# An adaLN + S4D + token-mixing block on one core: the first token block's late values come from SBUF, squares are taken from the sum, and the last gate moves to the activation

## The chip, the core and the metric

The kernel runs on one core of a Trainium2 chip. The metric is the device time of one execution, in microseconds; the runs shown for a kernel give a median. Engines are named as in the profile: PE (TensorE, with PEld for its weight loads), DVE (VectorE), ACT (ScalarE), POOL (GpSimd) and SP (SyncE). SPq is the queue of DMAs that SP issues.

## What is computed

All arrays are float32. `x` has 2048 tokens of 448 channels. The part of the reference that matters here:

```
mod = (_silu(c) @ w_mod)...          # six rows of 448: sa, ca, ga, sb, cb, gb
h = _layernorm(x) * (1 + ca) + sa
x = x + ga * _A_ref(h, ...)          # per-channel long convolution, by FFT
h = _layernorm(x) * (1 + cb) + sb
x = x + gb * _B_ref(h, ...)          # token mixing

def _B_ref(x, w1, b1, w2, b2):
    h = _layernorm(x, axis=-1)                  # again, over channels
    u = _gelu(einsum("bsd,sf->bdf", h, w1) + b1)   # 2048 tokens -> 1792
    y = einsum("bdf,fs->bds", u, w2) + b2          # 1792 -> 2048 tokens
    return y.transpose(0, 2, 1)
```

So there are two layer norms in a row for each token (the modulated one, then the plain one of `_B_ref`), and `gb` multiplies the output of the second product, bias included.

## The kernel before

**Stages.** The convolution is done with DFTs of length 4096, factored as 64 x 64, as matmuls. The kernel generation and the transforms of the input fill the first half of the time. What matters here is the end of the second stage and all of the third.

**End of stage two (lines 763 to 828 and 1170 to 1200).** The spectrum is multiplied and transformed back in 32 pieces `n = 0..31`. Pieces 0 to 15 make the first half of the channels (224 columns, `DC`), pieces 16 to 31 the second half. Each piece gives two of the 32 rows `k` of a table `v_d` in DRAM, `[32, 128, 448]`. For one piece: `pc_load` loads the signal's spectrum `u` and a table `si`; `pc_s2` is two matmuls (`kx`); `pc_mul` multiplies on DVE (`z`); `pc_inv` is four matmuls with the inverse tables (`vv`, L820 and L821); `pc_out` copies `vv` from PSUM to an SBUF tile `vt` on ACT (L826) and writes it to `v_d` (L828). In the loop at L1172, `pc_out` of piece `n - 1` follows the matmuls of piece `n`.

The 128 partitions of a piece's `vv` are 128 combinations of the token index. The tables `I1`, `I2` of `dft_tables` fix their order; before, it is `(ch, g, r)` with `ch` of 4, `g` of 2 and `r` of 16.

**Stage three, first product (L1203 to L1328).** Tokens are handled in 16 blocks `r` of 128. `ln_load(r)` loads from `v_d` what belongs to block `r` (a tile `vt` of 128 partitions, which are the 32 rows `k` and 4 `ch`, by 2 `g` by 448; L1230). `ln_y(r)` is the last transform, two matmuls with the table `ft` into PSUM tile `y` (L1250; there is one such buffer), and adds it to the residual on DVE with the row sum as by-product (L1253, `total`). `stats` gives the mean on DVE (L1240), the sum of squared differences on ACT (L1242, `Square` with the negated mean as bias) and the root on ACT (L1243). `ln_mod` applies the first norm and the modulation on DVE (L1260 to L1262), calls `stats` again, and `ln_out` applies the second norm (L1267 to L1280). Its result is split in two float32r tiles, `h3h` and `h3l`, whose sum is the value. `mlp1` multiplies them with the weights, also split (`whi`, `wlo`): three matmuls for each of seven slices of 128 hidden units (L1222 to L1224), into seven PSUM accumulators. That is done for the first 896 hidden units (parts 0 to 15) and then for the other 896 (parts 16 to 31).

**Weights.** `WeightStream` brings each part of the weights: `load` issues the raw load on SP (three raw buffers), `begin` casts it to `whi` on ACT (L206), `rest` makes `wlo` on DVE (L215). Parts 0 and 1 are prepared at L1199, before the first block is touched; their instructions stand ahead of block 0's in the queues of ACT and DVE.

**After each half (`gelu`, L1332).** Seven times: gelu on ACT from the accumulator into a tile `u` (three buffers; L1336), a cast to `uh` on DVE (L1337), the remainder `ul` on DVE (L1338).

**Second product (L1353 to L1370).** For each of 16 blocks of tokens, 42 matmuls into `o`, those on the first half's `uh` and `ul` first (L1364 to L1366). Then DVE adds `b2` and multiplies by `mod[5]`, which is `gb` (L1368), adds the residual (L1369), and SP stores the block.

**Order.** On PE, ACT, DVE and POOL the order is the written order in all that is described here. SP's queue is ordered by a planner until L1188, which is passed after piece 27 has been written; from there to L1328 its DMAs, too, are issued in the written order. A DMA that has to wait holds up those behind it on the same queue. Matmuls on `mod[3]` that nothing reads (`warm`) stand before each of the first three steps of the loop at L1296: nine, one and two.

## Time and profile before

| | us |
|---|---|
| median of 3 runs | 700.01 |
| the runs | 700.01, 697.52, 702.35 |
| the profiled execution's own time | 699.5 |
| its span, first to last instruction | 697.7 |
| PE busy in it | 646.5 |
| ACT, DVE, POOL busy | 448.5, 424.1, 274.7 |
| mean granted TensorE clock | 0.988 |
| DMA, over the span | 128.04 MB, 184 GB/s |

A row of the timeline reads: start, duration (us), engine, line, operation, tiles written and read, shape, count, and in brackets how long the engine was idle before and what ended that. In the chain of waits a row is start, duration and what took it; a DMA row runs from its issue to its landing. In a row of the windows the first number after the stretch is its length, then come the busy times of PE, PEld, DVE, ACT and POOL, the granted clock, the busy share of the DMA engines and the GB/s moved. A float32 matmul shows as two records.

### The profile page before, as it was taken

The page shows a single profiled execution, that of the slowest core. Times are in us where ns is not written, and L with a number is a line of the kernel's source. Part 1 is how long each engine was busy: PE and PEld are TensorE (multiplying, and loading weights), DVE is VectorE, ACT ScalarE, POOL GpSimd, SP SyncE. Part 2 cuts the span into 40 slices and gives each one's busy share as a digit, 9 for nine tenths or more (in the row PEclk, how much of TensorE's full clock was granted, in tenths as well). Part 3 has the DMA queues.
Part 4 walks back from the last instruction along what each step waited for, and adds up shares of the span by engine and source line. Part 5 has one row for each costly group of instructions (what it writes and reads, how often), then busy time and mean ns, then how long its engine had stood idle before and what let it go on. Part 6 is the DMA issues. An engine that isn't in the chain of part 4 may idle for free.

```text
span 697.7 us, 18532 instructions
## 1 busy us (share of the span) xinstructions
PE 646.5 (93%) x7314; PEld 486.1 (70%) x7314; DVE 424.1 (61%) x811; ACT 448.5 (64%) x841; POOL 274.7 (39%) x364
## 2 busy tenths in 40 slices
PE   0868999999988899999999989999999999999997
PEld 0444454455545676676789747778999999999996
DVE  7877889787575584857744368777622354444431
ACT  5787698899879899999766568877422332222220
POOL 6694669588588767777546200000000000000000
PEclk9998999999999999999999999999999999999999
DMA  7595647588785486554579899974683445555640
GB/s 183 178 194 143 214 163 241 212 234 268 213 266 165 126 170 170 145 157 120 142 235 301 257 278 244 236 177 135 174 247 108 146 132 159 159 158 165 169 129 28
DMA packets 101894, 128.04 MB, mean 184 GB/s; under 512 B 13547, under 2 KB 85231, under 8 KB 101807
## 3 DMA queue, kind: packets, MB, share of 16 engines
q1 hardware_dynamic: 100606, 123.31, 63.0%
q0 software_dynamic: 1200, 3.54, 2.4%
q8 instruction: 58, 0.95, 0.6%
q14 instruction: 30, 0.24, 0.1%
HBM read 91.46 MB, written 34.87 MB: 181 GB/s over the span
## 4 chain that ended last, share of the span: by engine, by line
PE 68%; ACT 10%; DMA 8%; DVE 6%; issue 4%; POOL 3%; SPq 1%; DVEq 0%; ACTq 0%; POOLq 0%
PE xe L621 7%; PE acc L1222 7%; PE o L1365 6%; PE o L1364 6%; PE o L1366 6%; PE acc L1223 6%; PE acc L1224 6%; PE kg L711 6%; DMA si<-in_SK_dram 3%; PE xg L621 3%; PE pu L542 2%; PE pu L574 2%; PE vv L820 2%; PE kx L804 2%; PE vv L821 2%
## 5 line engine op out<-in xcount | busy, mean ns | idle before, releaser
L206 ACT CAST whi<-w 128x896 fp32r<-128x896 f32 x64 | 59.8, 938 | 134.9 <-PE o L1365 84.6
L215 DVE TENSOR_TENSOR wlo<-w,whi 128x896 fp32r<-128x896 f32 x64 | 68.1, 1088 | 43.1 <-ACT whi L206 36.8
L684 POOL TENSOR_TENSOR G<-mag,gs 128x512 f32<-128x512 f32 x56 | 71.9, 1283 | 50.9 <-ACT gs L680 47.1
L1222 PE MATMUL acc<-h3h,whi 128*128 128x448 f32 x224 | 82.7, 369 | 0.8 <-ACT h3h L1273 0.8
L1223 PE MATMUL acc<-h3l,whi 128*128 128x448 f32 x224 | 81.5, 364 | 0.7 <-DVE h3l L1280 0.5
L1365 PE MATMUL o<-ul,whi 128*128 128x448 f32 x224 | 81.3, 363 | 0.0
L1364 PE MATMUL o<-uh,whi 128*128 128x448 f32 x224 | 81.2, 362 | 0.0
L1224 PE MATMUL acc<-h3h,wlo 128*128 128x448 f32 x224 | 80.7, 360 | 0.0
L1366 PE MATMUL o<-uh,wlo 128*128 128x448 f32 x224 | 80.6, 360 | 0.0
L711 PEld LDWEIGHTS kg<-E,G 128*32 128x32 f32 x3584 | 56.6, 114 | 32.3 <-issue 22.2
L711 PE MATMUL kg<-E,G 128*32 128x64 f32 x3584 | 66.4, 228 | 6.7 <-issue 6.1
L685 POOL TENSOR_TENSOR G<-mag,gs 128x512 f32<-128x512 f32 x56 | 71.8, 1282 | 0.0
L621 PE MATMUL xg<-tab,lph 64*128 64x512 f32 x112 | 62.3, 556 | 5.1 <-ACT gs L680 2.4
L621 PE MATMUL xe<-tab,lph 64*128 64x512 f32 x112 | 62.2, 555 | 1.1 <-ACT gs L681 0.9
L686 DVE TENSOR_TENSOR E<-m,xe 128x512 f32<-128x512 f32 x53 | 36.4, 687 | 41.3 <-ACT xe L679 24.3
L1368 DVE SCALAR_TENSOR_TENSOR y<-o,b,mod 128x448 f32<-128x448 f32 x16 | 10.9, 684 | 80.2 <-PE o L1366 80.2
L665 POOL TENSOR_TENSOR m<-mag,w 128x512 f32<-128x512 f32 x53 | 56.0, 1056 | 4.3 <-DMA u<-us_d 0.2
L1222 PEld LDWEIGHTS acc<-h3h,whi 128*128 128x128 f32 x224 | 42.0, 188 | 13.9 <-ACT h L1278 5.6
L812 DVE TENSOR_TENSOR z<-kx,u 128x448 f32<-128x448 f32 x48 | 28.4, 620 | 27.7 <-PE kx L804 27.7
L1223 PEld LDWEIGHTS acc<-h3l,whi 128*128 128x128 f32 x224 | 42.1, 188 | 3.3 <-DVE h3l L1280 0.8
L1364 PEld LDWEIGHTS o<-uh,whi 128*128 128x128 f32 x224 | 42.0, 188 | 3.4
L621 PE MATMUL xe<-tab,lex 64*128 64x512 f32 x56 | 28.9, 531 | 16.6 <-DMA lex<-wm 15.8
(233 smaller groups left out, 1512.1 us busy)
## 6 DMA issues: line engine op xcount, KB each, us to landing
w<-in_B_w_dram SPq DMA_DIRECT2D x64, 224.0 KB
w<-in_B_w_dram SPq DMA_DIRECT2D x32, 448.0 KB
u<-us_d SPq DMA_DIRECT2D x48, 224.0 KB
yu_d<-yt SPq DMA_DIRECT2D x16, 448.0 KB
yi<-yu_d SPq DMA_DIRECT2D x32, 224.0 KB
us_d<-uo SPq DMA_DIRECT2D x16, 448.0 KB
v_d<-vt SPq DMA_DIRECT2D x32, 224.0 KB
vt<-v_d SPq DMA_DIRECT2D x16, 448.0 KB
```

The lines of the kernel that those rows point to most:

```text
L206: self.nc.scalar.copy(hi, w)
L215: eng.tensor_tensor(lo, w, hi.bitcast(F32), ALU.subtract)
L621: T.matmul(out[k], lhs[r], rhs[r], start=start, stop=stop)
L684: G.tensor_tensor(Gt[:, 1], mg_, v32(sg), ALU.mult)
L685: G.tensor_tensor(Gt[:, 0], mg_, v32(cg_), ALU.mult)
L711: T.matmul(kg[32 * q : 32 * q + 32, m], Gt[:, c, d], E[:, c, d], start=h == 0 and c == 0 and m == 0, stop=h == 1 and c == 1, skip_group_ch ...
L1222: nc.tensor.matmul(acc[f], hi[:, fs], h3h[:, r], start=r == 0, stop=False)
L1223: nc.tensor.matmul(acc[f], hi[:, fs], h3l[:, r], start=False, stop=False)
L1224: nc.tensor.matmul(acc[f], lo[:, fs], h3h[:, r], start=False, stop=r == 15)
L1364: nc.tensor.matmul(o, hi[:, ks], uh[kh][:, k], start=kh == 0 and k == 0, stop=False)
L1365: nc.tensor.matmul(o, hi[:, ks], ul[kh][:, k], start=False, stop=False)
L1366: nc.tensor.matmul(o, lo[:, ks], uh[kh][:, k], start=False, stop=kh == 1 and k == 6)
```

## The change

There are four parts.

1. *The order of a piece's rows.* `I1` and `I2` are permuted so that the partitions of `vv` are `(r, ch, g)`. The eight rows of one block and one `k` now lie side by side in `v_d`, and the load of a block reads, for each partition, two neighbouring rows in one run (`v_load`).
2. *Block 0.* Its `vt` is loaded in stage two, in parts: two small loads bring the first-half columns of rows `k = 28..31` after piece 28 has been written (they lie there since pieces 14 and 15); at the loop's step 15 a load brings all columns of rows 0 to 27, which includes piece 29, and stands on SP before the writes of pieces 30 and 31. The second-half columns of rows 28 to 31 come from the SBUF tiles of pieces 30 and 31: four small copies, issued on ACT, put them in `vlast` (16 partitions). `ln_y(0)` becomes six matmuls of 224 columns: two over 128 rows, two over 112 rows, and two with the table `fl` over the 16 rows of `vlast`. `ln_load(0)` at the start of stage three is gone. The warm-up matmuls become two, three and one.
3. *Squares from the sum.* `Square` takes the sum as bias and scales its input by -448, so that the result is 448 squared times as large; `Sqrt` scales back. The mean is still made on DVE, and is no longer an input of the square.
4. *The gate.* `u` is multiplied by `mod[5]` on DVE right after each gelu. In the second half the cast to `uh` moves to ACT, one slice late. After the second product, `b2 * mod[5]` and the residual are joined without `o`, and `o` is added last.

```diff
-    order = lambda a: a.reshape(P, 32, 2, 2, 2, 16).swapaxes(3, 4)
+    order = lambda a: a.reshape(P, 32, 2, 2, 2, 16).transpose(0, 1, 5, 2, 4, 3)
...
+    t["FL"] = ft[-16:].reshape(2, 2, 4, 64).swapaxes(1, 2).reshape(16, 64)
...
             nc.sync.dma_start(rows.rearrange("k p d -> p k d"), vt)
+            if n >= 2 * NP - 2:
+                q = 8 * (n % 2)
+                for g in range(2):
+                    nc.scalar.dma_start(vlast[q : q + 8, g], vt[g:8:2])
...
+        v_v = v_d.rearrange("k (r ch g) d -> r k ch g d", ch=4, g=2)
+        end = 2 * NP - 4
+        vlast = swp.tile([16, 2, DC], F32, name="vlast", bufs=1)
+        fl = swp.tile([16, 64], F32, name="fl", bufs=1)
+        nc.sync.dma_start(fl, i["FL"])
+        vts = {}
+
+        def v_load(r, k):
+            nc.sync.dma_start(vts[r][0 : 4 * k].rearrange("p g d -> p (g d)"), v_v[r, 0:k].rearrange("k ch g d -> k ch (g d)"))
...
+            if k == NP - 1:
+                v_load(0, end)
             if k:
                 pc_inv(n - 1)
                 pc_out(n - 1)
...
             if k == NP - 3:
                 wst.load()
                 x_pair(0)
+                vts[0] = rot.tile([P, 2, D], F32, tag="vt", name="vt", bufs=4)
+                for g in range(2):
+                    nc.sync.dma_start(vts[0][4 * end :, g, 0:DC], v_v[0, end:, :, g, 0:DC])
...
-        v_v = v_d.rearrange("k (ch g r) d -> r (k ch) g d", ch=4, g=2)
...
-            nc.sync.dma_start(vts[r], v_v[r])
+            v_load(r, 2 * NP)
...
-            V.tensor_scalar(mean, total, -1.0 / D, None, ALU.mult)
             sq = rot.tile([P, D], F32, tag="sq", name="sq")
-            S.activation(sq, src, AF.Square, bias=mean, accum_out=ss)
-            S.activation(rs, ss, AF.Sqrt, scale=1.0 / D, bias=eps_t)
+            S.activation(sq, src, AF.Square, bias=total, scale=-float(D), accum_out=ss)
+            S.activation(rs, ss, AF.Sqrt, scale=1.0 / D**3, bias=eps_t)
+            V.tensor_scalar(mean, total, -1.0 / D, None, ALU.mult)
...
+                if r:
+                    nc.tensor.matmul(out, ft, vt[:, g], start=True, stop=True)
+                    continue
+                n = 4 * end
+                nc.tensor.matmul(out[:, 0:DC], ft, vt[:, g, 0:DC], start=True, stop=True)
+                nc.tensor.matmul(out[:, DC:], ft[0:n], vt[0:n, g, DC:], start=True, stop=False)
+            if r == 0:
+                for g in range(2):
+                    nc.tensor.matmul(y[64 * g : 64 * g + 64, DC:], fl, vlast[:, g], start=False, stop=True)
...
-        for r in range(4):
+        for r in range(1, 4):
             ln_load(r)
...
-                warm((9, 1, 2)[t + 3])
+                warm((2, 3, 1)[t + 3])
...
         def gelu(acc, fh):
+            us = {}
+
+            def split(f, copy):
+                copy(uh[fh][:, f], us[f])
+                V.tensor_tensor(ul[fh][:, f], us[f], uh[fh][:, f].bitcast(F32), ALU.subtract)
+
             for f in range(7):
                 k = 7 * fh + f
-                u = ru.tile([P, D], F32, tag="u", name="u")
-                S.activation(u, acc[f], AF.Gelu_apprx_tanh, bias=b1[:, k : k + 1])
-                V.tensor_copy(uh[fh][:, f], u)
-                V.tensor_tensor(ul[fh][:, f], u, uh[fh][:, f].bitcast(F32), ALU.subtract)
+                us[f] = ru.tile([P, D], F32, tag="u", name="u")
+                S.activation(us[f], acc[f], AF.Gelu_apprx_tanh, bias=b1[:, k : k + 1])
+                V.tensor_tensor(us[f], us[f], mod[5], ALU.mult)
+                if fh == 0:
+                    split(f, V.tensor_copy)
+                elif f:
+                    split(f - 1, S.copy)
+            if fh:
+                split(6, S.copy)
...
-            V.scalar_tensor_tensor(y, o, b2[:, t : t + 1], mod[5], ALU.add, ALU.mult)
-            V.tensor_tensor(y, y, xt, ALU.add)
+            V.scalar_tensor_tensor(xt, mod[5], b2[:, t : t + 1], xt, ALU.mult, ALU.add)
+            V.tensor_tensor(y, o, xt, ALU.add)
```

9 lines of the change are left out of this document (5 added, 4 removed).

## The prediction

> **What bounds the kernel now.** I read the page first, then the chain of waits, and then the timeline engine by engine between 384 and 420 us, where the second stage hands over to the mixer block.
>
> ```profile
> PE 646.5 (93%) x7314; PEld 486.1 (70%) x7314; DVE 424.1 (61%) x811; ACT 448.5 (64%) x841; POOL 274.7 (39%) x364
> PE 68%; ACT 10%; DMA 8%; DVE 6%; issue 4%; POOL 3%; SPq 1%; DVEq 0%; ACTq 0%; POOLq 0%
> L1223 PE MATMUL acc<-h3l,whi 128*128 128x448 f32 x224 | 81.5, 364 | 0.7 <-DVE h3l L1280 0.5
> ```
>
> TensorE has 93% of the span and 68% of the chain. In the group row of the mixer's second product, 224 matmuls were preceded by 0.7 us of idle in all (behind the bar): once it has started, PE hardly waits. So a change pays only in the handover and after the last matmul, and costs wherever it makes PE wait anew.
>
> ```profile
> 384.81 4.63 DMA si<-in_SK_dram
> 392.78 0.38 PE vv L820 x2
> 394.17 3.22 DMA v_d<-vt
> 394.20 7.03 PE L1294 MATMUL acc<-mod 128*128 128x448 f32 x18 [0.67 <-ACT vt L826]
> 401.37 0.97 PE L1250 MATMUL y<-vt,ft 128*64 128x448 f32 x4
> 406.67 0.97 PE L1250 MATMUL y<-vt,ft 128*64 128x448 f32 x4 [0.77 <-DVE xt L1253]
> 408.49 0.47 PE L1222 MATMUL acc<-h3h,whi 128*128 128x448 f32 x1 [0.85 <-ACT h3h L1273]
> 416.39 0.48 PE L1223 MATMUL acc<-h3l,whi 128*128 128x448 f32 x1 [0.54 <-DVE h3l L1280]
> ```
>
> Stage two's last matmuls end 0.67 before 394.20. The write of piece 31 starts at 394.17 and lands 3.22 us later; the block's load then brings row block 0 by 401.37, nine warm-up matmuls filling the time. After `y(0)` comes a chain over DVE and ACT, and the mixer's first matmul starts at 408.49. Between 408.49 and 416.86 PE still waits 0.54 us for `h3l` of block 1.
>
> **The handover on SyncE.** SP takes its DMAs here in written order.
>
> ```profile
> 389.29 1.24 SPq L1166 DMA_DIRECT2D xt<-in_A_u_dram  x2
> 390.63 3.90 SPq L828 DMA_DIRECT2D v_d<-vt  x3
> 394.58 1.65 SPq L186 DMA_DIRECT2D w<-in_B_w_dram  x2
> 397.47 1.22 SPq L1230 DMA_DIRECT2D vt<-v_d  x2
> 400.03 1.25 SPq L1230 DMA_DIRECT2D vt<-v_d  x2
> L335 SPq DMA_DIRECT2D dskr<-in_A_D_skip_dram x4: 220/240/475, 5.4 to 7.1; - x4
> 397.00:398.00 1.00, 1.00 (x4) 0.51 (x3) 0.61 (x1) 0.00 (x0) 0.00 (x0) 1.00 1.05 319
> ```
>
> The three writes are pieces 29, 30 and 31; the first starts at 390.63. The new order is: two small loads of first-half columns, write 29, the load of 28 pieces for block 0, write 30, write 31, the raw `w` load, then block 1's load. The 28-piece load must wait until write 29 has landed, and while it waits, writes 30 and 31, the `w` load and every later load stand behind it.
>
> Each small load costs SP between 0.24 (the issue of a one-row load, row L335) and 0.6 (half of 1.22); I take 0.4, so write 29 starts at 391.4. It lands after 3.22 us (the write above, few transfers beside it) to 4.63 us (the `si` load at 384.81, DMA queues full). Write 29 has two `w` and two `xt` loads just before it, so I take 4.0: 395.4, with 394.3 (391.1 + 3.22) and 396.4 (391.8 + 4.63) as ends. Then come 0.6 for the 28-piece load and two writes of 0.4 with gaps, 1.5 together: the `w` load starts at 396.9 (395.8 to 397.9) where it started at 394.58.
>
> What hangs on it is not `y(0)` but the second weight piece, which is cast on ACT and subtracted on DVE ahead of block 0's first step:
>
> ```profile
> 399.36 0.94 ACT L206 CAST whi<-w 128x896 fp32r<-128x896 f32 x1 [2.87 <-DMA w<-in_B_w_dram]
> 400.39 1.09 DVE L215 TENSOR_TENSOR wlo<-w,whi 128x896 fp32r<-128x896 f32 x1 [2.77 <-ACT whi L206]
> 402.39 0.62 DVE L1253 SCALAR_TENSOR_TENSOR xt<-xt,y 128x448 f32<-128x448 f32 x1 [0.92 <-DMA vt<-v_d]
> ```
>
> The cast waited for the `w` load, 4.78 us after that load's start, and the subtraction ended at 401.48, 2.12 later. In the new order this becomes 396.9 + 4.78 = 401.7 if the queues are as free as before. The 28-piece load puts 28/32 of 448 KB, 401,000 bytes, ahead of it: at the 319 GB/s of the window row that is 1.26 us more, 402.9. I take the middle, 402.3. Cast and subtraction end at 404.4, and L1253 starts there instead of at 402.39: **+2.05** (ends +0.35 and +3.7).
>
> [...]
>
> `y(0)` itself is early enough. Its load takes about the 3.9 us from 397.47 to 401.37: 395.4 + 3.9 = 399.3. It becomes six matmuls of 224 columns, twelve records at 0.19 (0.38 for two, chain row at 392.78), 2.3 us instead of 0.97: done at 401.6, covered by the 404.4 above. Without that cover the gain would be at most 402.34 − 401.6 = 0.7 us. The four copies into `vlast` start on ACT behind the two casts of `vv`; at 0.6 each and 4.63 to land they are there by 400, and on ACT they fall before the 2.87 us that it idled. Rows of 3584 bytes instead of 1792 halve the pieces of each block load; the loads after 417 keep no one waiting, so I count nothing.
>
> **Squares from the sum.** The mean drops out of the chain before each square; DVE still makes it beside ACT.
>
> ```profile
> 402.94 0.08 DVE L1253 DVE_READ_ACCUMULATOR xt<-xt,y 128x1 f32 x1
> 403.29 0.67 ACT L1242 ACTIVATE sq<-xt,mean 128x448 f32<-128x448 f32 x1 [3.00 <-DMA xt<-in_A_u_dram]
> 405.81 0.08 DVE L1262 DVE_READ_ACCUMULATOR h<-h,rs,mod 128x1 f32 x1
> 406.11 0.67 ACT L1242 ACTIVATE sq<-h,mean 128x448 f32<-128x448 f32 x1 [1.73 <-DVE mean L1240]
> 409.19 0.67 ACT L1242 ACTIVATE sq<-xt,mean 128x448 f32<-128x448 f32 x1 [0.76 <-DVE mean L1240]
> ```
>
> The sum is out at 403.02 and the square starts at 403.29; the second time 405.89 and 406.11. With a gap of 0.04 kept, this saves 0.23 + 0.18: **−0.4** for the first matmul, which so comes at 408.49 + 1.65 = 410.1. For block 1 the square at 409.19 waited 0.76 for a mean that sat behind `h3l` on DVE. That wait goes, and most of the 0.54 at 416.39 with it: **−0.5**; from then on DVE's own queue is next.
>
> **The gate at the activation.** The product with `mod[5]` adds one DVE instruction to each of 14 slices.
>
> ```profile
> 488.08 2.49 ACT L1336 ACTIVATE u<-acc,b 128x448 f32<-128x448 f32 x4 [2.27 <-PE acc L1224]
> 492.81 0.64 ACT L1336 ACTIVATE u<-acc,b 128x448 f32<-128x448 f32 x1 [0.33 <-DVE ul L1338]
> 488.75 0.39 DVE L1337 CAST uh<-u 128x448 fp32r<-128x448 f32 x1 [2.42 <-ACT u L1336]
> 489.18 0.63 DVE L1338 TENSOR_TENSOR ul<-u,uh 128x448 fp32r<-128x448 f32 x1
> 489.72 0.39 DVE L1337 CAST uh<-u 128x448 fp32r<-128x448 f32 x1
> 495.50 3.09 DVE L215 TENSOR_TENSOR wlo<-w,whi 128x896 fp32r<-128x896 f32 x3
> 495.24 0.20 PE acc L1222
> 555.28 2.49 ACT L1336 ACTIVATE u<-acc,b 128x448 f32<-128x448 f32 x4 [4.06 <-PE acc L1224]
> L1279 ACT CAST h3h<-h x15: 565/567/571, 414.3 to 483.1; 128x448 fp32r<-128x448 f32 x15
> ```
>
> In the first half, DVE's turn per slice was 0.97 (488.75 to 489.72). A product of that shape costs 0.63 (as the subtraction) and 0.03 before the cast that needs it: 1.63. Only three `u` buffers exist, so gelu 6 waits for subtraction 3: the first ends at 488.75 + 0.66 + 0.43 + 0.63 = 490.47, the fourth at 495.36. With the 0.12 seen before 492.81, gelu 6 runs 495.48 to 496.12. When does PE want that accumulator? Matmuls come every 0.20 (chain row at 495.24), three to a slice. The first gelu started at 488.08, when slice 0's last matmul was done; that one had begun 0.4 earlier, at 487.7, the next group's slice 0 follows 3.8 later and its seventh slice 3.6 after that: 495.1. The stall is 496.12 − 495.1 and a gap: **+1.1** (0.3 if the product overlaps as the cast does, 1.9 if the backlog also delays the `wlo` that followed at 495.50). DVE would end its seven slices at 500.25, and that `wlo` at 501.3 is just in time for its use near 501.4.
>
> In the second half the cast goes to ACT, 0.62 (a quarter of 2.49) + 0.57 a slice, against two of 0.63 on DVE. Starting at 555.28 both are through by 564.5 or so (seven slices of 1.2 and one pass of 0.6). PE goes to the last product 3.4 after that start, 558.7; 21 matmuls on the first half's `uh` fill 4.2, and the last slice is wanted 3.6 later, at 566.5. About 2 us of cover: nothing; without it, each 1 us of backlog is 1 us.
>
> **The tail.**
>
> ```profile
> 693.28 0.68 DVE L1368 SCALAR_TENSOR_TENSOR y<-o,b,mod 128x448 f32<-128x448 f32 x1 [7.05 <-PE o L1366]
> 694.00 0.63 DVE L1369 TENSOR_TENSOR y<-y,x 128x448 f32<-128x448 f32 x1
> ```
>
> Bias and residual are joined while PE works; one step remains after the last matmul: **−0.7**.
>
> **Sum.** +2.05 − 0.4 − 0.5 + 1.1 − 0.7 = +1.55. The profiled execution took 699.5 us (span 697.7 and 1.8 around it), so 701.0; the median of the runs lies 0.5 above that execution: **701.5**. With the ends of the unknown terms, 699 to 704.
>
> **Rivals.** *The short handover works.* If write 29 lands in 3.22 and the `w` load comes at its early end, the first term is +0.35 and the total 699.8. If SP's wait cost nothing at all, L1253 would start at 401.5, behind the unmoved `wlo`: −0.9, −0.4, −0.5, −0.7, and with a free gelu step −2.5, which is 697.5. For it speaks that few transfers stood beside the 3.22; against it that write 29 has four loads ahead. [...] Chance 0.25, about 698.7.
>
> *The clock drops.* This is the slower side. Warm-up matmuls go from nine to two before `y(0)`; at 0.78 each (7.03 for nine) they end at 395.8 and PE stands until 399.3.
>
> ```profile
> 217.00:220.36 3.36, 2.25 (x67) 1.40 (x67) 3.06 (x5) 3.33 (x7) 3.19 (x4) 1.00 0.11 39
> 220.36:223.77 3.41, 3.41 (x97) 2.74 (x100) 0.71 (x2) 2.53 (x6) 2.54 (x4) 0.50 0.83 205
> 404.68:408.09 3.41, 2.19 (x8) 0.51 (x6) 2.65 (x9) 1.47 (x4) 0.00 (x0) 1.00 1.09 322
> ```
>
> PE was busy 2.25 of 3.36 us, and the next 3.41 us ran at half clock; yet 2.19 of 3.41 at 404.68 brought no drop. By the new times the last 3.4 us before the mixer hold `y(1)`, `y(2)` and one warm-up matmul: 2.7 us, or 1.75 where one of the `y` falls outside. If the drop falls on the mixer's first 3.4 us, 1.7 are lost: 703.2. A drop on `y(0)` alone hides under the 404.4. [...] Chance 0.15.
>
> *The loads of blocks 1 and 2 come late.* Block 1's load needs write 31, which starts near 396.5 and lands near 401; block 2's load starts 2 us later at 403, against 400.03. `y(2)` ran at 406.67, at most 6.64 after its load's start, so by 409.6 now, and it stands before the mixer's first matmul at 410.1 on PE. If the queues are 1.5 us fuller than that, it decides: 702.5 to 703.5. Chance 0.10.
>
> **Numbers.** The forecast has 0.5. The range takes in the rivals' ends, and the spread of the three runs (697.52 to 702.35): 697 to 705. One per cent, 7 us, is about what a measurement can tell from no change: below 693 needs a gain that no row offers, 0.02; above 707 needs clock and late loads together with the far ends, 0.04; within, 0.94.
>
> **What would show it.** On SP an idle of about 3.5 us before the 28-piece load; the raw `w` load starting near 396.9 and its cast near 402.3; L1253 right behind `wlo` near 404.4; the first mixer matmul near 410; no wait of the squares for a mean; a PE stall of about 1 us at the seventh accumulator after the first gelu; one DVE step after the last matmul. The forecast is wrong if `w` lands by 400, if the granted clock is 0.5 anywhere between 398 and 415, or if PE waits in the mixer for anything else.

## The result, and the profile after

| | before | changed |
|---|---|---|
| median, us | 700.23 | 702.82 |
| runs, lowest to highest | 20, 697.36 to 705.31 | 20, 699.62 to 706.66 |
| profiled execution's own time | 699.5 | 701.28 |
| its span | 697.7 | 699.5 |

The ratio is 1.0041, with a 95% interval of 1.0023 to 1.0059. That is 2.9 us (0.0041 of 700.23), slower by less than one per cent; the forecast was 701.5 in a range of 697 to 705.

The page of the changed kernel: busy time by engine, the shares of the chain that ended last, and the groups of the mixer's first two products (busy us, mean ns, then the idle time ahead of them).

```profile
PE 644.3 (92%) x7310; PEld 484.5 (69%) x7310; DVE 428.7 (61%) x818; ACT 451.2 (65%) x848; POOL 274.5 (39%) x364
...
PE 71%; ACT 10%; DMA 6%; DVE 6%; issue 4%; POOL 1%; SPq 1%; ACTq 0%; DVEq 0%; POOLq 0%
...
L1242 PE MATMUL acc<-h3h,whi 128*128 128x448 f32 x224 | 82.8, 369 | 1.1 <-ACT u L1371 0.7
L1243 PE MATMUL acc<-h3l,whi 128*128 128x448 f32 x224 | 81.4, 364 | 0.2 <-DVE mean L1263 0.2
```

DVE has 4.6 us more work (the gate products, less the casts that went to ACT), PE none. The wait for `h3l` ahead of the second product is gone, and a new one of 0.7 us for a gelu stands ahead of the first.

**Where to measure from.** Stages one and two end anywhere between 388.5 and 397.8 us in the executions shown here, so times of two kernels can't be set side by side as they stand. From here on they count from the end of the last matmul of stage two, called E: 392.99 + 0.54 = 393.53 before, 391.72 + 0.54 = 392.26 in the changed kernel. The timeline of PE, changed kernel:

```profile
391.72 0.54 PE L823 MATMUL vv<-z,si 128*128 128x224 f32 x2
394.23 1.77 PE L1323 MATMUL acc<-mod 128*128 128x448 f32 x4 [1.97 <-ACT vt L828]
400.23 1.02 PE L1275 MATMUL y<-vt,ft 128*64 128x224 f32 x4 [4.23 <-DMA vt<-v_d]
401.00 1.00 PE L1276 MATMUL y<-vt,ft 112*64 112x224 f32 x4
401.93 1.01 PE L1279 MATMUL y<-vlast,fl 16*64 16x224 f32 x4
402.87 4.22 PE L1323 MATMUL acc<-mod 128*128 128x448 f32 x6
...
410.25 0.48 PE L1242 MATMUL acc<-h3h,whi 128*128 128x448 f32 x1 [0.41 <-ACT h3h L1302]
```

`y(0)` starts at E + 7.97 (before: 401.37, E + 7.84). So the values of block 0 came no earlier, though two of the pieces no longer went through HBM. The mixer starts at E + 17.99 (before 408.49, E + 14.96): three microseconds went between these two points. From E to the end of the span it is 307.2 us in place of 304.2.

SP's timeline, changed kernel:

```profile
386.92 1.22 SPq L188 DMA_DIRECT2D w<-in_B_w_dram  x2
388.18 1.24 SPq L1172 DMA_DIRECT2D xt<-in_A_u_dram  x2
389.53 2.57 SPq L1213 DMA_DIRECT2D vt<-v_d  x2
392.52 0.36 SPq L830 DMA_DIRECT2D v_d<-vt  x1
395.31 0.87 SPq L1185 DMA_DIRECT2D vt<-v_d  x1
396.28 1.00 SPq L830 DMA_DIRECT2D v_d<-vt  x2
397.33 1.36 SPq L188 DMA_DIRECT2D w<-in_B_w_dram  x2
401.45 0.54 SPq L1185 DMA_DIRECT2D vt<-v_d  x1
```

And SP's waits in the same kernel between 380 and 412 us (total, number, longest):

```profile
SPq L1185 <- DMA v_d<-vt: 5.1, 2, 2.7
...
SPq L1213 <- DMA w<-in_B_w_dram: 1.2, 1, 1.2
```

The two small loads (L1213) take SP 2.57 us, of which the profile puts 1.2 down to a wait for the landing of a `w` load that they don't use. Write 29 (392.52, E + 0.26) is then 3.2 us later than before (E − 2.90). The 28-piece load waits for its landing; writes 30 and 31, the raw `w` load (E + 5.07, before 1.05) and block 1's load (E + 9.19, before 4.55) come behind; write 30, whose copy on ACT had ended at 391.32, is issued at 396.28.

On ACT and on DVE of the changed kernel (two timelines):

```profile
391.35 2.20 ACTq L834 DMA_DIRECT2D vlast<-vt  x2
393.65 0.53 ACT L828 COPY vt<-vv 128x448 f32<-128x448 f32 x1 [2.33 <-issue]
...
403.74 0.67 ACT L1261 ACTIVATE sq<-xt,sum 128x448 f32<-128x448 f32 x1 [5.84 <-DVE xt L1282]
...
404.40 0.92 ACT L208 CAST whi<-w 128x896 fp32r<-128x896 f32 x1
405.23 0.29 ACT L1262 ACTIVATE rs<-ss,eps_t 128x1 f32<-128x1 f32 x1
```

```profile
403.07 0.62 DVE L1282 SCALAR_TENSOR_TENSOR xt<-xt,y 128x448 f32<-128x448 f32 x1 [4.05 <-PE y L1279]
...
405.36 1.09 DVE L217 TENSOR_TENSOR wlo<-w,whi 128x896 fp32r<-128x896 f32 x1 [1.47 <-ACT whi L208]
406.37 0.15 DVE L1289 RECIPROCAL rs<-rs 128x1 f32<-128x1 f32 x1
...
408.04 0.62 DVE L1282 SCALAR_TENSOR_TENSOR xt<-xt,y 128x448 f32<-128x448 f32 x1
...
408.99 0.16 DVE L1298 RECIPROCAL rs<-rs 128x1 f32<-128x1 f32 x1 [0.32 <-ACT rs L1262]
```

The cast and the subtraction of the second weight part are no longer ahead of block 0's sum (L1282), although the description of the kernel above has every engine in the written order; that does not hold for these two instructions. They stand in the middle of its chain: the cast between the square and `rs`, the subtraction between `rs` and the reciprocal that needs it. The square's sum is read by 404.49; without the two, `rs` would have run at 404.53 and the reciprocal at about 404.85 instead of 406.37. That is 1.5 us on this chain, but not on the mixer's start. Block 1's sum (408.04 to 408.66) stands on DVE ahead of block 0's last step (L1298, 408.99). It waits for `y(1)`, which PE makes only behind the six warm-up records (402.87 to 407.09; `y(1)` runs from 407.02 to 407.99). With the 1.5 us gone, L1298 could have started at about 408.6, which is 0.4 us sooner: two paths of nearly the same length end there.

The windows around the idle of PE, changed kernel (length, busy times of PE, PEld, DVE, ACT, POOL, granted clock, DMA share, GB/s):

```profile
396.00:399.49 3.49, 0.00 (x1) 0.00 (x0) 1.15 (x2) 1.88 (x3) 0.00 (x0) 1.00 0.65 169
399.49:402.90 3.41, 2.67 (x13) 1.21 (x13) 0.00 (x0) 0.00 (x0) 0.00 (x0) 0.50 0.74 222
402.90:406.32 3.42, 3.42 (x7) 1.78 (x6) 1.75 (x4) 1.78 (x4) 0.00 (x0) 0.50 0.95 271
```

After a stretch of 3.49 us without a matmul the clock is halved for 6.83 us. This is `y(0)`, which took 2.71 us (400.23 to 402.94), and the six warm-up records behind it.

### The profile page after: what moved, and what is told of

It reads as the page before. It is cut to its first block, busy times and chain, and to the rows that moved or that the text cites. A ratio compares the mean times of both kernels' runs of the same rounds, so it can differ in the third digit from the quotient of the medians.

```text
span 699.5 us, 18530 instructions
## 1 busy us (share of the span) xinstructions
PE 644.3 (92%) x7310; PEld 484.5 (69%) x7310; DVE 428.7 (61%) x818; ACT 451.2 (65%) x848; POOL 274.5 (39%) x364
## 4 chain that ended last, share of the span: by engine, by line
PE 71%; ACT 10%; DMA 6%; DVE 6%; issue 4%; POOL 1%; SPq 1%; ACTq 0%; DVEq 0%; POOLq 0%
PE xe L623 7%; PE o L1406 6%; PE acc L1242 6%; PE o L1405 6%; PE o L1404 6%; PE acc L1243 6%; PE acc L1244 6%; PE kg L713 6%; PE kx L806 3%; PE vv L822 2%; PE xg L623 2%; PE pu L544 2%; PE vv L823 2%; DMA si<-in_SK_dram 2%; PE pu L576 2%
## 5 line engine op out<-in xcount | busy, mean ns | idle before, releaser
L1409 DVE TENSOR_TENSOR y<-o,x 128x448 f32<-128x448 f32 x16 | 10.0, 625 | 78.9 <-PE o L1406 78.9
L1242 PEld LDWEIGHTS acc<-h3h,whi 128*128 128x128 f32 x224 | 42.0, 187 | 14.5 <-ACT h L1307 3.5
L1405 PEld LDWEIGHTS o<-ul,whi 128*128 128x128 f32 x224 | 42.0, 188 | 3.4
```

What stands on the lines that cost most here:

```text
L1242: nc.tensor.matmul(acc[f], hi[:, fs], h3h[:, r], start=r == 0, stop=False)
L1405: nc.tensor.matmul(o, hi[:, ks], ul[kh][:, k], start=False, stop=False)
```

## The experiments

One table for all, from each run's profiled execution. E is in us from the span's start, the other columns are us from E: the first matmul of `y(0)`, its length, the start of block 0's sum on DVE, the mixer's first matmul, the end of the last matmul, the end of the span. The last column is the time at half clock in the handover. Ratios are to the kernel before, with 95% intervals.

| kernel | ratio | E | y(0) | takes | sum | mixer | last | span | half |
|---|---|---|---|---|---|---|---|---|---|
| before | 1 | 393.53 | 7.84 | 0.97 | 8.86 | 14.96 | 299.71 | 304.2 | 0 |
| changed | 1.0041 (1.0023 to 1.0059) | 392.26 | 7.97 | 2.71 | 10.81 | 17.99 | 303.17 | 307.2 | 6.8 |
| 1 no block 0 | 0.9978 (0.9950 to 1.0006) | 388.50 | 8.40 | 0.97 | 9.42 | 15.15 | 300.35 | 304.3 | 0 |
| 2 block 0 only | 1.0039 (1.0016 to 1.0062) | 390.47 | 7.28 | 2.71 | 10.12 | 17.73 | 302.55 | 307.1 | 6.8 |
| 3 small loads early | 1.0078 (1.0048 to 1.0107) | 391.60 | 7.36 | 2.54 | 10.03 | 17.36 | 302.61 | 306.7 | 6.8 |
| 4 copies on GpSimd | one run | 393.21 | 7.98 | 2.71 | 10.82 | 18.75 | 304.01 | 307.6 | 10.2 |
| 5 seven warm-ups | 1.0024 (0.9998 to 1.0051) | 389.59 | 8.30 | 1.51 | 9.94 | 17.43 | 303.00 | 307.1 | 0 |
| 6 load behind writes | 1.0032 (1.0011 to 1.0054) | 392.00 | 8.34 | 3.17 | 11.65 | 19.67 | 304.93 | 309.0 | 10.2 |
| 7 and more on GpSimd | 1.0057 (1.0035 to 1.0080) | 390.25 | 8.11 | 2.98 | 11.22 | 17.85 | 304.05 | 308.1 | 6.8 |
| 8 no block 0, gelu on ACT | 0.9975 (0.9947 to 1.0003) | 389.34 | 8.19 | 0.97 | 9.21 | 14.92 | 298.95 | 302.7 | 0 |
| 9 gate only | 1.0017 (0.9985 to 1.0048) | 391.53 | 8.21 | 0.97 | 9.23 | 15.32 | 301.21 | 305.2 | 0 |
| 10 loads earlier | 0.9992 (0.9963 to 1.0021) | 397.79 | 4.60 | 2.85 | 7.54 | 14.77 | 300.01 | 303.8 | 6.8 |
| 11 and clock, gelu on ACT | 0.9999 (0.9967 to 1.0030) | 391.53 | 4.83 | 1.89 | 6.81 | 14.89 | 298.92 | 302.5 | 0 |
| 12 and wlo on DVE | 0.9979 (0.9953 to 1.0006) | 393.88 | 4.63 | 2.49 | 7.21 | 14.36 | 298.12 | 301.7 | 0 |

### What each part costs: runs 1, 2 and 9

Run 1 is the changed kernel without its part on block 0: all pieces' values from HBM, warm-up counts as before, squares from the sum and the gate kept.

```diff
-            if n >= 2 * NP - 2:
...
-                    nc.scalar.dma_start(vlast[q : q + 8, g], vt[g:8:2])
...
-            if k == NP - 1:
-                v_load(0, end)
...
-                    nc.sync.dma_start(vts[0][4 * end :, g, 0:DC], v_v[0, end:, :, g, 0:DC])
...
-        for r in range(1, 4):
+        for r in range(4):
...
-                warm((2, 3, 1)[t + 3])
+                warm((9, 1, 2)[t + 3])
```

> The change without block 0's own path: block 0 is loaded with the others at the start of stage three, y(0) is two matmuls, warm-up matmuls are nine, one and two; the new row order, the squares from the sum and the gate at the activation stay. Theory A (block 0's path costs about 3 us between the last matmul of stage two and the mixer's first, the other parts gain about 0.9 + 0.7 and give back 0.7): ratio to the kernel before 0.9987 (0.997 to 1.000), mixer start about 0.9 us earlier than before, counted from the last matmul of stage two. Theory B (the row order or the gate costs the time, block 0's path is even): ratio 1.002 or more.

Run 2 keeps the part on block 0 and takes the other two back.

```diff
-            S.activation(sq, src, AF.Square, bias=total, scale=-float(D), accum_out=ss)
+            S.activation(sq, src, AF.Square, bias=mean, accum_out=ss)
...
-                V.tensor_tensor(us[f], us[f], mod[5], ALU.mult)
...
-            V.scalar_tensor_tensor(xt, mod[5], b2[:, t : t + 1], xt, ALU.mult, ALU.add)
-            V.tensor_tensor(y, o, xt, ALU.add)
+            V.scalar_tensor_tensor(y, o, b2[:, t : t + 1], mod[5], ALU.add, ALU.mult)
+            V.tensor_tensor(y, y, xt, ALU.add)
```

> The other half: the kernel before with the new row order and block 0's path alone, squares and gate as before. Theory A: about 3.0 + 0.4 us more than before in the handover (no gain from the means), 1.0050 (1.0035 to 1.007). Theory B: 1.001 or less.

Run 9 is the kernel before with the gate part alone.

```diff
+                V.tensor_tensor(us[f], us[f], mod[5], ALU.mult)
...
-            V.scalar_tensor_tensor(y, o, b2[:, t : t + 1], mod[5], ALU.add, ALU.mult)
-            V.tensor_tensor(y, y, xt, ALU.add)
+            V.scalar_tensor_tensor(xt, mod[5], b2[:, t : t + 1], xt, ALU.mult, ALU.add)
+            V.tensor_tensor(y, o, xt, ALU.add)
```

> The kernel before with the gate part of the change alone (gate product at the activation, the tail's bias step ahead of the last matmul); block 0 and the squares as before. Theory A: TensorE waits 0.7 us for ScalarE at the seventh accumulator of the first half, and the tail is 0.4 us shorter; the time from the mixer's start to the last matmul is 284.7 plus 0.7, so 285.4 us, the tail 4.0, and the ratio is 1.000 to 1.001. Theory B (the wait comes only with the mixer's later start): no such wait, and the ratio is 0.999 to 1.000.

The block-0 part alone has all of the loss: ratio 1.0039 against 1.0041, mixer at E + 17.73. Without it the kernel is no slower than before. In run 1 the way from the sum to the mixer is 5.73 us (15.15 − 9.42) in place of 6.10: the 0.4 of the squares. Its mixer was expected 0.9 earlier than before and came 0.19 later, since `y(0)` came 0.56 later, behind a wait of 0.70 for its load. The new row order doesn't explain that wait: run 9 has the old order and waits 0.51. The gate alone comes out at 1.0017 with an interval from 0.9985 to 1.0048, which doesn't tell its two theories apart by time; but its wait is there without any late mixer, so theory B of that run falls. From the mixer's start to the last matmul run 9 takes 285.89 us, 1.14 more than before and more than the 285.4 expected. PE's longest wait for a gelu in run 9 after 380 us:

```profile
PE acc L1222 <- ACT u L1342: 0.7, 1, 0.7
```

The cost is larger than this wait. Between the first gelu of one half and the first of the next it is 67.20 us before, 68.35 in run 9 and in the changed kernel: 1.15 more. PE's timeline of the changed kernel shows why:

```profile
496.04 0.37 PE L1244 MATMUL acc<-h3h,wlo 128*128 128x448 f32 x1
497.15 0.47 PE L1242 MATMUL acc<-h3h,whi 128*128 128x448 f32 x1 [0.74 <-ACT u L1371]
```

Matmuls start every 0.20 us here, though each is drawn 0.36 long. The idle time counts from the end of the drawn bar; from start to start it is 1.11, which is 0.91 too long. Another 0.2 lies in two starts that came 0.30 and 0.31 after the one before them in place of 0.20: those behind the first matmul of the sixth slice (495.53) and of the seventh (497.15).

### The gelu wait: run 8

Run 8 is run 1 with the cast of the gate product on ACT, one slice late, in the first half too.

```diff
-                if fh == 0:
-                    split(f, V.tensor_copy)
-                elif f:
+                if f:
                     split(f - 1, S.copy)
-            if fh:
-                split(6, S.copy)
+            split(6, S.copy)
```

> The changed kernel without its part on block 0 (all 32 pieces' values from HBM as before the change, squares from the sum and the gate product kept), and the cast of the gate product on ScalarE one slice late in the first half too, as the second half has it. Theory A (the 0.7 us that TensorE waits for ScalarE at the seventh accumulator of the first half comes from DVE's 1.6 us a slice, with gate product, cast and remainder): that wait falls below 0.2 us, the time from the mixer's start to the last matmul falls from 285.2 us to about 284.5, and the ratio is 0.997 (0.998 with that cast on DVE). Theory B (the wait is ScalarE's own, one more cast there makes it longer): the wait stays at 0.7 us or grows to over 1 us, and the ratio is 0.998 to 1.000.

Among PE's waits in run 8 after 395 us there is none for a gelu any more; the longest is 0.7 us for block 0's `h3h`. From the mixer's start to the last matmul it is 284.03 us, 1.17 less than in run 1 (285.20), which is the whole 1.15 of the gate in the first half. Theory A holds. The ratio, 0.9975, is as forecast, and its interval just reaches 1.

### The handover: runs 3, 4, 5, 6 and 7

Run 3 issues the two small loads before the loop of stage two.

```diff
+        vts[0] = rot.tile([P, 2, D], F32, tag="vt", name="vt", bufs=4)
+        for g in range(2):
+            nc.sync.dma_start(vts[0][4 * end :, g, 0:DC], v_v[0, end:, :, g, 0:DC])
         pc_swap(NP)
```

> The whole change, with the two small loads of block 0 issued before piece 16 instead of after piece 28, so that write 29 no longer stands behind them on SP. Theory A (the write of piece 29 and the 28-piece load behind it set y(0)): write 29 is issued some 3 us earlier against the last matmul of stage two, but its bytes still go behind the w and xt loads, so it lands about 1.1 us earlier and so does everything to the mixer's start: ratio about 1.0025. Theory C (the halved clock and the longer y(0) set the handover, not SP): 1.0041 as the change itself.

SP's timeline of run 3:

```profile
387.69 1.24 SPq L1172 DMA_DIRECT2D xt<-in_A_u_dram  x2
389.02 0.53 SPq L830 DMA_DIRECT2D v_d<-vt  x1
394.17 0.90 SPq L1185 DMA_DIRECT2D vt<-v_d  x1
```

Write 29 is back at E − 2.58, and the load behind it still starts only at E + 2.57: the write now needs 5.15 us from issue to the load's release (in the changed kernel 2.79, 392.52 to 395.31). So the small loads aren't the cause by themselves. In time the run missed both theories (1.0078; the mixer starts 0.63 earlier where A had 1.1); its profiled execution is not slower than the changed kernel's (306.7 against 307.2 from E), and why its timed runs were is not known.

Run 4 issues the copies into `vlast` on GpSimd.

```diff
-                    nc.scalar.dma_start(vlast[q : q + 8, g], vt[g:8:2])
+                    nc.gpsimd.dma_start(vlast[q : q + 8, g], vt[g:8:2])
```

> The changed kernel with the four copies of the last pieces' values into vlast issued by GpSimd instead of ScalarE. Theory A (of the 3 us that the handover costs, most stands on SP's order, and ScalarE's copy issues add a little): copy 31 (L828), which in the changed kernel starts 1.39 us after the last stage-two matmul because two copy issues of 2.20 us stand ahead of it, starts about 0.1 us after that matmul; the 28-piece load is issued no earlier, at about 3.0 us after it, and the mixer starts at about 17 to 18 us after it. Theory B (ScalarE's copy issues are what holds the handover): the mixer starts 1.3 us earlier, at about 16.7 us.

Copy 31 starts at 393.29, E + 0.08, and the load of 28 pieces still at E + 3.25: theory A, though the mixer, at E + 18.75, is later than the 17 to 18 it gave, with a half clock of 10.2 us. The chain of waits of the changed kernel names a copy into `vlast` as what released that load; here, with those copies on another queue, SP waits 3.5 us for the write alone, so the write is taken as the cause.

Run 5 has seven warm-up products ahead of `y(0)`, the kernel otherwise as changed.

```diff
-                warm((2, 3, 1)[t + 3])
+                warm((7, 3, 1)[t + 3])
```

> The whole change with seven warm-up matmuls before y(0) instead of two, so that PE does not stand for 4.2 us before it. Both theories: granted clock 1.0 throughout. Theory A: only y(0)'s own loss goes, 2.76 to 2.3 us, 0.5 us in all: ratio about 1.0034. Theory C (the clock is the main loss): 1.5 us or more, ratio 1.002 or less.

The interval of the ratio holds both theories, so the trace has to tell. The clock stays up, `y(0)` takes 1.51 us in place of 2.71, and the sum comes 0.9 us earlier. The mixer comes only 0.56 earlier, and from E to the span's end nothing is left (307.1). PE's waits in run 5 say what took its place, the loads of the next blocks:

```profile
PE y L1272 <- DMA vt<-v_d: 3.2, 3, 1.3
...
PE y L1275 <- DMA vt<-v_d: 1.0, 1, 1.0
```

The half clock is thus real and mostly covered, which is nearer to theory A. One more thing was seen here: the warm-up count alone moved the second weight part's cast behind `rs` and its subtraction behind the two modulation steps. That order is not written; it is set by the planner that orders the instructions ahead of the mixer, where the kernel fixes no order for ACT and DVE. So the 0.56 us is not the clock's alone.

Run 6 moves the 28-piece load and the small loads behind the writes of pieces 30 and 31.

```diff
-            if k == NP - 1:
-                v_load(0, end)
...
+        vts[0] = rot.tile([P, 2, D], F32, tag="vt", name="vt", bufs=4)
+        v_load(0, end)
+        for g in range(2):
+            nc.sync.dma_start(vts[0][4 * end :, g, 0:DC], v_v[0, end:, :, g, 0:DC])
         wst.load()
         last.close()
```

> The changed kernel with the 28-piece load and the two loads beside it moved on SP behind the writes of pieces 30 and 31 and ahead of the raw weight load. Theory A (the load and the two small ones hold up the two writes, the raw weight load and all later loads of SP, and gain nothing for block 0): the writes come at about -0.9 and 0.6 us after the last stage-two matmul as before the change, the load at about 2 us, the raw weight load at about 4 us, the mixer starts at about 15.5 to 16.5 us in place of 18.0, and the ratio to the kernel before is 0.999 to 1.002 in place of 1.0041. Theory B (SP's order is not it; the y product in two pieces and the moved cast are): the mixer start stays within 0.5 us of 18.0 and the ratio at 1.003 to 1.005.

Run 7 is run 6 with the `vlast` copies and the second `wlo` on GpSimd.

```diff
-            wst.ahead(n + 1, nc.vector, False)
+            wst.ahead(n + 1, (nc.vector, nc.gpsimd)[n], False)
```

> As the run with the load behind the writes, and besides it the copies into vlast issued by GpSimd and the remainder (wlo) of the second weight part on GpSimd. Theory A: copy 31 is no longer held by 1.35 us, and wlo no longer stands in DVE's chain from block 0's sum to the mixer (0.8 us); the mixer starts some 1 to 2 us earlier than in that run, at about 14.5 to 15.5 us, and the ratio is 0.997 to 1.000. Theory B (ScalarE's and DVE's extra work lies beside the waits for the loads): no earlier than in that run by more than 0.3 us, same ratio within 0.001.

Both miss theory A; run 7's mixer is 1.82 us earlier than run 6's, as its theory A had it, but far from its 14.5 to 15.5, and its ratio is no lower. The writes did come early (E − 1.95, 0.03 and 1.68 in run 6), but the load then started at E + 3.66 and the mixer at E + 19.67, the latest of all. DVE's timeline in run 6 shows where the rest went:

```profile
406.94 0.15 DVE L1262 TENSOR_SCALAR mean<-sum 128x1 f32<-128x1 f32 x1
409.86 0.62 DVE L1281 SCALAR_TENSOR_TENSOR xt<-xt,y 128x448 f32<-128x448 f32 x1 [2.77 <-PE y L1271]
...
410.41 0.16 DVE L1297 RECIPROCAL rs<-rs 128x1 f32<-128x1 f32 x1
```

Block 0's last steps (L1297) stand on DVE behind block 1's sum, which waits for `y(1)`; `y(1)` stands on PE behind six warm-up records, and these took 4.85 us at half clock. `rs` for that reciprocal had been done at 408.02. So the half clock is covered only as long as the waits for loads are longer.

With A fallen, the theory became this (Q): the load is released by the landing of write 29, and that write moves on the queue behind the 0.9 MB (four transfers of 224 KB) of `w` and `xt` loads issued just ahead of it. The traces above already speak for it. Where SP had been done with those loads for longer when it issued the write, the write released its reader sooner (5.15 us after its issue right behind them, 2.42 and 2.79 with some 3 us between):

| kernel | from the end of the last bulk issue to the write's issue, us | from the write's issue to the release, us |
|---|---|---|
| 3 | 0.1 | 5.15 |
| 4 | 1.6 | 3.98 |
| 5 | 2.9 | 2.42 |
| changed | 3.1 | 2.79 |

So in all four the release comes 5.2 to 5.9 us after the last bulk load was issued, whenever the write was; in runs 6 and 7 it is 5.7 and 5.6. That is why taking the small loads away brought only 0.5 us (run 3) while the bulk loads stood where they were.

### The repair: runs 10, 11 and 12

Run 10 writes those four loads one piece earlier, with the small loads before the loop, the `vlast` copies and the second `wlo` on GpSimd.

```diff
-            if k == NP - 3:
+            if k == NP - 4:
                 wst.load()
                 x_pair(0)
```

> The changed kernel with four moves: the first weight load and the first pair of x loads are issued on SP one piece earlier (behind write 27 instead of behind write 28), the two small loads before the loop, the copies into vlast on GpSimd, and the remainder of the second weight part on GpSimd. Theory Q (write 29 moves on the DMA queue behind 0.9 MB of weight and x loads issued just ahead of it, and its landing is what starts the 28-piece load, so that block 0's values come no sooner than before the change): write 29 is issued at about -2.9 us from the last stage-two matmul and lands 2.5 us later, the 28-piece load is issued at -0.5 to 0.5 us in place of 3.0, the first product of y(0) starts at 4 to 5 us in place of 8.0, the mixer starts at 12 to 14 us in place of 18.0 (before the change 15.0), and the ratio to the kernel before is 0.996 to 0.999. Theory R (a load from HBM waits some 3 us for the landing of a write whatever else is on the queue): the 28-piece load stays at 2.5 us or later, the mixer starts at 16.5 us or later, and the ratio is 1.002 or more.

SP's timeline in run 10:

```profile
357.18 2.24 SPq L188 DMA_DIRECT2D w<-in_B_w_dram  x2
...
390.33 1.23 SPq L1172 DMA_DIRECT2D xt<-in_A_u_dram  x2
...
392.86 2.24 SPq L830 DMA_DIRECT2D v_d<-vt  x2
397.24 0.91 SPq L1185 DMA_DIRECT2D vt<-v_d  x1
```

In the trace only the two `xt` loads come one piece earlier. The two `w` loads, written beside them at the border of the part where SP's order is fixed, were issued at 357.18, 33 us ahead of them, and so in runs 11 and 12; that is not what was meant, and why is not shown. So half of the 0.9 MB is gone from in front of the write, and the other half is 3.2 us ahead of it. Write 29 is the second of the two; its issue of 0.36 ends at 395.10 and so began at 394.74, E − 3.05. The load follows at 397.24, E − 0.55, where R wanted 2.5 or later. `y(0)` starts at E + 4.60 in place of 7.97. So R falls. That the bulk loads were what stood in the way agrees with the table above, but this run alone doesn't show it, since it made four moves at once: the small loads (run 3) and the copies on GpSimd (run 4) had each been moved without the release coming before E + 2.5, but no run moved both without the bulk loads. The mixer, at E + 14.77, is later than the 12 to 14 of Q: the half clock (6.8 us) is still there, `y(0)` takes 2.85 us and six warm-up records 4.64. The ratio, 0.9992, lies just above Q's 0.996 to 0.999. Here the weight part is no longer inside block 0's chain, and still the way from its sum to the mixer is 7.23 us: DVE waits for block 1's sum. Two rows, of DVE's timeline and of the windows:

```profile
410.76 0.62 DVE L1282 SCALAR_TENSOR_TENSOR xt<-xt,y 128x448 f32<-128x448 f32 x1 [1.98 <-PE y L1272]
```

```profile
399.40:402.69 3.29, 1.12 (x7) 0.36 (x7) 1.15 (x2) 1.33 (x3) 0.44 (x1) 0.99 0.92 273
```

The second shows the stretch ahead of the half clock: PE was busy for 1.12 of its 3.29 us and its longest idle was 2.17, so here the clock fell without an idle time as long as the 3.49 us ahead of the half clock in the changed kernel.

Run 11 adds five warm-up products in place of two and run 8's cast on ACT.

```diff
-                warm((2, 3, 1)[t + 3])
+                warm((5, 3, 1)[t + 3])
```

> The run with the loads one piece earlier, and besides it five warm-up products instead of two ahead of block 0 and the cast of the gate product on ScalarE, one slice late, in the first half too. Theory Q (the values of block 0 now come early, and what is left of the handover's cost is the half clock: y(0) in 3.0 us, six warm-up matmuls in 4.6 us, behind them y(1), and behind its sum on DVE the last step of block 0): the granted clock stays at 1 through the handover, y(0) takes 1.6 us, the mixer starts at about 13 us after the last stage-two matmul in place of 14.8, the wait for ScalarE at the seventh accumulator is gone, the time from the mixer's start to the last matmul is 284.1 us, and the ratio to the kernel before is 0.994 to 0.997. Theory L (the loads of blocks 1 to 3, behind the writes of pieces 30 and 31, are the next bound, as in the run with seven warm-up products): the mixer starts at 14 us or later or TensorE waits over 1 us for them inside the mixer, and the ratio is 0.997 to 1.000.

The clock stays at 1, the gelu wait is gone, the mixer's part takes 284.03 us; the mixer itself starts no earlier, at E + 14.89, and the ratio is 0.9999. Theory L has the time, but only part of the cause: `y(1)` waits 1.27 us for its load. DVE's and GpSimd's timelines of run 11:

```profile
400.82 0.16 DVE L1289 RECIPROCAL rs<-rs 128x1 f32<-128x1 f32 x1 [1.66 <-ACT rs L1262]
400.90 2.38 DVE L1290 SCALAR_TENSOR_TENSOR h<-xt,mean,mod 128x448 f32<-128x448 f32 x1
```

```profile
400.74 2.07 POOL L217 TENSOR_TENSOR wlo<-w,whi 128x896 fp32r<-128x896 f32 x1 [7.14 <-ACT whi L208]
```

DVE's step L1290, 0.67 us in the changed kernel, took 2.38 and ended 0.47 after GpSimd's subtraction. That was a cost of this repair's own, and run 7 had it as well (1.20 us).

Run 12 puts the second `wlo` back on DVE, and writes its place and that of its cast by hand.

```diff
             if t == -2:
+                part1 = wst.begin(2)
                 ln_mod(0)
+                wst.rest(part1, V, False)
```

> The run before, with the remainder (wlo) of the second weight part back on DVE, set in DVE's order behind block 0's two modulation steps, and its cast (whi) in ScalarE's order behind block 0's first rs. Theory G (in the run before, GpSimd's subtraction of 2.4 us slowed DVE's modulation step from 0.67 to 2.38 us, and whi stood 0.5 us ahead of rs; both lie in block 0's chain): that step takes 0.67 us again, block 0's sum to the mixer's first product takes 6.5 us in place of 8.1, the mixer starts at about 13.4 us after the last stage-two matmul in place of 14.9, held there by y(1), whose values load only behind the landing of write 31; ratio 0.993 to 0.998. Theory L (y(1) and the loads behind it set the mixer's start anyway): the start stays at 14.5 us or later, ratio 0.997 to 1.001.

The step takes 0.67 us again, so that part of G is shown; from the sum to the mixer it is 7.15 us, not its 6.5. The mixer starts at E + 14.36, between the two theories, and PE's timeline says why it is not 13.4:

```profile
400.07 0.93 PE L1278 MATMUL y<-vlast,fl 16*64 16x224 f32 x4 [0.57 <-DMA vlast<-vt]
...
404.39 0.97 PE L1271 MATMUL y<-vt,ft 128*64 128x448 f32 x4 [0.94 <-DVE h L1290]
...
407.34 0.97 PE L1271 MATMUL y<-vt,ft 128*64 128x448 f32 x4 [1.04 <-DMA vt<-v_d]
```

`y(0)` waits 0.57 for the `vlast` copies from GpSimd, and `y(2)`, the last product ahead of the mixer, 1.04 for its load. From E to the span's end run 12 has 301.7 us, the least of all, 1.0 less than run 8 without the block-0 part; the timed runs (0.9979 and 0.9975) don't tell the two apart, and both intervals just hold 1. So even repaired, the block-0 part can't be shown to gain anything.

## Why the prediction came out as it did

The forecast of 701.5, a little slower, held with 702.82; its sum was +1.55 where the runs show +2.6 to +3.0. Term by term, forecast against one profiled execution of each kernel:

| term | forecast | measured |
|---|---|---|
| block 0's sum starts later | +2.05 | +1.95 (8.86 to 10.81) |
| from the sum to the mixer's first matmul | −0.4 | +1.08 (6.10 to 7.18) |
| from there to the last matmul: squares | −0.5 | −0.72 (79.59 to 78.87, to the first gelu) |
| the same: gate | +1.1 | +1.15 (67.20 to 68.35, from gelu to gelu) |
| tail | −0.7 | −0.4 (4.5 to 4.1) |

**The handover, +2.05.** The size is right and the path to it is not. The forecast took the sum to be held by the `w` load, its cast and `wlo`, and `y(0)` to lie in their cover. In the run it is `y(0)` that holds the sum, as the bracket of L1282 says. So the agreement of this term is luck: two errors cancel. SP was later than forecast, with the raw `w` load at E + 5.07 where 396.9 is E + 3.37; and the weight part that was to hold the sum had gone behind it. Three steps before `y(0)` were off. The small loads, set at 0.4 us each, took 2.57 together with a wait, so that write 29 came at E + 0.26 and not at 391.4 (E − 2.1). The 28-piece load needed 4.9 us to the first product (395.31 to 400.23), not 3.9. And `y(0)`, set at 2.3 us, took 2.71 at half clock; at full clock it is 1.51 (run 5), so the twelve records were priced too high, which hid part of the halving.

**From the sum to the mixer, −0.4 against +1.08.** This is the term that was wrong, by 1.5 us, and it makes the difference between the forecast sum and the measured one. Two things took its place, and by the rows either alone would have cost most of it.

- The order of the second weight part, "cast on ACT and subtracted on DVE ahead of block 0's first step". In the changed kernel both stand behind it, inside the chain, for 1.5 us. Runs 5 and 12 show that this order can change with a warm-up count, or be written by hand. Kept ahead, they would have held the sum instead: with the forecast's own 4.78 us from the `w` load to its cast and 2.12 to the end of the subtraction, an estimate of 404.2 in place of the sum's 403.07.
- The half clock, by way of `y(1)`. The forecast looked at a drop on `y(0)` and at one on the mixer, and not at the warm-up records between them. These push `y(1)` to 407.02 and so block 1's sum, behind which block 0's last step waits on DVE. Without the 1.5 us the mixer would start about 0.4 sooner and no more, as worked out under the result, and run 10, where the weight part is out of the chain, still needs 7.23 us.

The expectation that ACT's copy issues fall into idle time failed too: two of them took 2.20 us and held the copy of piece 31 to E + 1.39. But with them gone (run 4) the load started no earlier, so they were not what decided.

**The clock.** By the prediction's own condition (0.5 anywhere between 398 and 415) its forecast of an undisturbed clock was wrong: that rival came true. Its price was not the 1.7 us of a halved mixer, since the drop fell on `y(0)` and the warm-up. What keeping the clock up won was 0.56 us at the mixer's start (run 5), with the loads as the next bound. What the clock alone costs in the changed kernel, with its order of instructions kept, no run shows.

**Late loads of blocks 1 and 2** didn't show in the changed kernel, since everything ahead of them was later too; with the clock kept up they became the next bound at once (run 5, 3.2 us).

**Squares from the sum.** Right in mechanism and size: 6.10 to 5.73 in run 1, and no wait for `h3l` of block 1 in the changed kernel (0.5 before). To the first gelu the mixer is 0.72 us shorter, a little more than the 0.5.

**The gate at the activation.** Right in mechanism and size. DVE's turn was 1.63 us as forecast, and the seventh accumulator was where PE waited. The row of waits says 0.7, but from gelu to gelu the price is 1.15, and run 8, which takes it away, gains 1.17. In the second half there was no wait, as forecast.

**The tail.** One DVE step of 0.62 after the last matmul, as forecast, 0.7 less; the store behind it took 3.4 us in place of 3.1, so that 0.4 is left in the span.

## What to carry to other kernels

A load that is moved ahead of the writes it doesn't need still waits for the last write it does need, and here that write released it 5.15 us after its issue right behind four bulk loads (run 3), and 2.42 us after it with 2.9 us between (run 5): look for bulk loads in front of such a write before cutting the last bytes out of the path (here 0.9 MB; in run 10, with half of it gone from there, the other half one piece earlier and two other moves, the block's values came 3.4 us sooner). When a first step is made early, follow the next two: here block 1's values, the clock and a weight cast stood right behind it and took back what was won. And where instructions outside a written order may be placed by a planner, their place beside a critical chain is to be fixed, or read in the new trace, before anything is hidden in it. The same holds for an experiment's edit: the trace says where the moved loads went.

## What the runs showed of the hardware

- A write to HBM took 5.15 us from its issue to the release of its reader right behind four loads of 224 KB (run 3, 389.02 to 394.17), 3.98 with 1.6 us between the last load's issue and the write's (run 4), and 2.4 to 2.8 with 2.9 to 3.2 us between (run 5, the changed kernel, and run 10 behind two of the loads, 394.74 to 397.24).
- DVE's `h = (xt + mean) * mod`, 0.67 us in the changed kernel, took 2.38 beside a GpSimd subtraction of 2.07 us (run 11), and 1.20 where the two overlapped less (run 7). Both times DVE's step ended some 0.5 us after GpSimd's instruction: at 403.28 after 402.81, and at 404.53 after 404.04.
- A DMA issue on ACT held that engine 0.64 to 1.51 us (the four copies into `vlast` in the changed kernel, the first two 2.20 us together), where those on SP in the same stretch took 0.36 (write 29) to 0.87 (the 28-piece load). On SP the profile shows an issue that waits for the landing of an earlier transfer that has nothing to do with it (1.2 us in the changed kernel, L1213 for a `w` load); why is not shown.
- The granted clock fell to 0.50 after 3.49 us without a matmul in the changed kernel, and in run 10 after a stretch in which PE was busy for 1.12 of 3.29 us. It stayed so for 6.8 us or for 10.2. In the first 3.4 us of the half clock PE was busy for 2.46 us (run 2), 2.53 (run 7), 2.67 (the changed kernel) and 3.41 (runs 3 and 10) where it lasted 6.8, and for 1.71 (run 4) and 2.36 (run 6) where it lasted 10.2. PE was busy all through the rest of it. Seven cases don't make a threshold.
